# Normaliser and output gate in transposed squares of 32 by 32, and a written order for every engine and the transfer queue, in an mLSTM cell followed by a SwiGLU block

## Chip, cores and metric

One Trainium2 chip, one core. The time is device time in microseconds (us). The kernel before takes 761.7 us in the median of the four runs beside the changed kernel (760.92 to 761.99). Engines: PE is the matrix engine, DVE the vector engine, ACT the scalar engine, POOL is GpSimd, and SP is the engine whose queue issues nearly all transfers.

## The reference

An mLSTM cell (4 batches, 8 heads, 768 steps, head size 40), then a SwiGLU block on its 3072 tokens of 320 numbers. Weights arrive as float64 and are cut to float32 on the chip.

```python
# cell, per step t (m, f_stab, i_stab: running maximum and stabilised gates)
C = f_stab * C + i_stab * outer(vt, kt)
n = f_stab * n + i_stab * kt
y[:, :, t] = sigmoid(o_gate) * (C @ qt) / maximum(abs(n . qt), 1.0)
# block
g = x @ w_gate
out = (g * sigmoid(g) * (x @ w_val)) @ w_out        # 320 -> 1536 -> 320
```

## The kernel before

Time is cut in chunks of 128 steps: 24 units (batch and chunk) in 8 groups of three. For each unit, PE transposes k and q (`turn`) and multiplies them (`scores`). A weight matrix `w` is loaded (a running maximum, spread over all partitions), turned into decay weights (`weigh`), multiplied by the scores, and used in `attend`. Each attention also makes the new state C, which the next one needs; q is scaled by loaded factors e before it meets C. The normalised, gated result `x` is stored to memory and read back transposed as `xT`, the input of the block. A group's block has a hidden phase (12 steps, `gv_ps`, PE's largest work) and nine projection parts (`o_ps`), between which the next group's three `attend` stand. That stretch is the boundary. Weights are converted in 18 pieces during the start and group 0: 12 for the hidden products, 6 for `w_out`.

```python
tc_order = ctx.enter_context(tc.manual_schedule(engines={PE}))   # only PE's order is the program's
...
    def weigh(u):
        w = un["w"] = work.tile([128, H, L], F32, name="w_sb", bufs=2 * GC - 1)
        nc.sync.dma_start(out=w, in_=M_dram[b][c].unsqueeze(0).to_broadcast([128, H, L]))
        nc.vector.tensor_tensor(w, gb, w, op=ALU.subtract)
        nc.gpsimd.affine_select(w, w, ...)          # causal mask
        nc.scalar.activation(w, w, AF.Exp)
    ...
    def attend(u):
        ...                                         # products onto ys (PSUM), new state C
        for two in range(2):
            nc.vector.stream_shuffle(r[:, part], ys[two], mask=[ONE] * 32)   # denominator to 32 rows
            nc.vector.tensor_tensor(x[:, part], ys[two], un["o"][:, part], op=ALU.mult)
        nc.scalar.activation(r, r, AF.Abs)
        nc.vector.tensor_scalar(r, r, scalar1=1.0, scalar2=None, op0=ALU.max)
        nc.vector.reciprocal(r, r)                  # 128x512
        nc.vector.tensor_tensor(x, x, r, op=ALU.mult)
        ...                                         # four stores of x, two transposed reads into xT
    ...
        for u in after:                             # group after next: before the boundary, in program order
            weigh(u)
        follow = {-1: [(attend, nxt[0])], 1: [(attend, nxt[1])], 3: [(attend, nxt[2])]}
        for n in range(-1, 3 * GC):
            if n >= 0:
                project(g, *divmod(n, 3))
            for f, u in follow.get(n, ()):
                f(u)
```

## Time and profile before

| stretch, from the timeline of PE | us |
|---|---|
| start to the first hidden product of group 0 | 90.3 |
| the same of group 1 | 227.3 |
| periods of groups 1 to 5 | 80.2, 80.6, 79.6, 80.0, 76.5 |
| group 1's first hidden product to the end | 533.6 |

Read it as two parts: an uneven start up to 227 us and regular groups after it. The table of stretches shows both (per engine the busy us and the number of instructions, then granted clock, mean busy share of the 16 transfer engines, GB/s):

```profile
core 0: us, PE busy (x) PEld busy (x) DVE busy (x) ACT busy (x) POOL busy (x), PEclk, DMA share, GB/s
...
90.00:227.00 137.00, 96.13 (x512) 64.43 (x512) 104.67 (x135) 41.86 (x57) 39.29 (x29) 0.81 0.61 143
227.00:307.00 80.00, 74.64 (x512) 52.39 (x512) 41.54 (x70) 22.25 (x34) 9.47 (x10) 0.95 0.35 79
```

### The profile page before, as it was taken

To read this page: it belongs to the slowest core of one execution; us is meant where nothing else is said; L and a number is where in the kernel's file an instruction comes from. 1 tells how busy PE (TensorE), PEld (TensorE's weight loads), DVE (VectorE), ACT (ScalarE), POOL (GpSimd) and SP (SyncE) were. 2 spreads that over 40 slices of the span, in tenths; PEclk is the share of its full clock that TensorE was granted. 3 is DMA by queue.
4 is the path that set the end of the run, shared out by engine and by line. 5 is a ranking of instruction groups with operands and counts; after the bars stand their busy time and mean duration, and the time that the engine had idled before them with its cause. 6 is when DMAs were issued, how large, how long until landed. Compare 5 with 4: busy or idle time off the path is not lost.

```text
span 760.9 us, 10611 instructions
## 1 busy us (share of the span) xinstructions
PE 626.6 (82%) x4104; PEld 440.0 (58%) x4104; DVE 425.9 (56%) x659; ACT 193.0 (25%) x291; POOL 118.9 (16%) x129
## 2 busy tenths in 40 slices
PE   3244393668769998899969998999699999997998
PEld 3233362435547676566746666887476666675665
DVE  4689546999953476346814493449444844391330
ACT  2512131422333133211521243113321231110110
POOL 3252112533210111110100111101100101000000
PEclk9655596678889999899979998999899999998999
DMA  7775757655470046402640166007500220012000
GB/s 118 180 148 101 175 92 161 162 145 158 80 171 19 28 93 146 98 22 68 144 100 15 46 136 155 29 15 155 142 1 29 79 70 28 1 45 60 1 1 26
DMA packets 159954, 65.50 MB, mean 86 GB/s; under 512 B 106240, under 2 KB 152672, under 8 KB 159904
## 3 DMA queue, kind: packets, MB, share of 16 engines
q1 hardware_dynamic: 159904, 64.83, 36.8%
q8 instruction: 32, 0.52, 0.3%
q14 instruction: 18, 0.15, 0.1%
HBM read 56.75 MB, written 8.04 MB: 85 GB/s over the span
## 4 chain that ended last, share of the span: by engine, by line
PE 63%; DVE 11%; issue 11%; DMA 6%; POOL 3%; SPq 3%; ACT 2%; DVEq 0%; POOLq 0%; ACTq 0%
PE gv_ps L363 38%; PE o_ps L378 16%; PE yT L303 3%; DVE r_sb L339 3%; PE tp_kq L270 2%; PE sp L281 2%; DMA w_sb<-M_dram 2%; PE add L318 1%; DMA raw<-in_moe_w_val_dram 1%; DMA o<-in_o_gate_dram 1%; DMA xT<-x_dram 1%; DVE wo_sb L228 1%; DVE size L234 1%; POOL wgv_sb L235 1%; DVE wgv_sb L231 1%
## 5 line engine op out<-in xcount | busy, mean ns | idle before, releaser
L363 PE MATMUL gv_ps<-xT,wgv_sb 64*128 64x384 f32 x1920 | 359.3, 517 | 69.6 <-DVE sg L367 27.8
L363 PEld LDWEIGHTS gv_ps<-xT,wgv_sb 64*128 64x128 f32 x1920 | 229.0, 201 | 186.5 <-issue 53.1
L367 DVE TENSOR_TENSOR sg<-sg,gv_ps 128x384 f32<-128x384 f32 x96 | 53.1, 553 | 209.7 <-ACT sg L366 209.7
L378 PE MATMUL o_ps<-wo_sb,h_sb 128*128 128x320 f32 x576 | 167.3, 443 | 0.0
L378 PEld LDWEIGHTS o_ps<-wo_sb,h_sb 128*128 128x128 f32 x576 | 107.7, 193 | 42.5 <-issue 3.0
L366 ACT ACTIVATE sg<-gv_ps 128x384 f32<-128x384 f32 x96 | 47.1, 491 | 240.4 <-PE gv_ps L363 240.4
L339 DVE RECIPROCAL r_sb<-r_sb 128x512 f32<-128x512 f32 x24 | 80.3, 3344 | 0.6
L369 DVE TENSOR_TENSOR h_sb<-sg,gv_ps 128x384 f32<-128x384 f32 x96 | 53.1, 553 | 9.6 <-DVE sg L367 0.5
L257 DVE TENSOR_TENSOR w_sb<-g_T,w_sb 128x1024 f32<-128x1024 f32 x24 | 30.7, 1280 | 48.9 <-DMA w_sb<-M_dram 48.9
L291 POOL TENSOR_TENSOR qT<-qT,e_bc 128x512 f32<-128x512 f32 x20 | 27.4, 1372 | 176.8 <-PE sp L281 176.8
L258 POOL TENSOR_SCALAR_AFFINE_SELECT w_sb<-w_sb 128x1024 f32<-128x1024 f32 x24 | 28.4, 1184 | 156.1 <-DVE w_sb L257 133.8
L260 ACT ACTIVATE w_sb<-w_sb 128x1024 f32<-128x1024 f32 x24 | 25.4, 1057 | 107.5 <-POOL w_sb L258 107.4
L281 PE MATMUL sp<-qT,kT 64*128 64x128 f32 x384 | 33.5, 281 | 7.6 <-DVE w_sb L284 7.6
L281 PEld LDWEIGHTS sp<-qT,kT 64*128 64x128 f32 x384 | 32.6, 194 | 11.7 <-DVE w_sb L284 7.8
L303 PE MATMUL yT<-w_sb,v 128*64 128x128 f32 x384 | 30.0, 304 | 10.9 <-DVE w_sb L284 10.9
L284 DVE TENSOR_TENSOR w_sb<-sp,w_sb 128x512 f32<-128x512 f32 x48 | 31.0, 682 | 4.7 <-POOL v_w L263 4.7
L303 PEld LDWEIGHTS yT<-w_sb,v 128*64 128x64 f32 x384 | 23.2, 151 | 17.1 <-DVE w_sb L284 11.6
L318 PE MATMUL add<-v_w,k 128*64 128x48 f32 x320 | 20.5, 241 | 13.6 <-DVE x_sb L336 10.2
L133 DVE STREAM_TRANSPOSE oT<-o 128x512 f32<-128x512 f32 x24 | 26.4, 1114 | 8.9 <-ACT o L131 8.8
L337 ACT ACTIVATE r_sb<-r_sb 128x512 f32<-128x512 f32 x24 | 15.0, 627 | 55.3 <-DVE r_sb L335 55.3
L318 PEld LDWEIGHTS add<-v_w,k 128*64 128x64 f32 x320 | 19.6, 154 | 15.1 <-DVE x_sb L336 11.3
L235 POOL TENSOR_TENSOR wgv_sb<-wgv_sb,size 128x640 f32<-128x640 f32 x12 | 19.7, 1640 | 52.6 <-DVE size L234 51.8
(68 smaller groups left out, 422.2 us busy)
## 6 DMA issues: line engine op xcount, KB each, us to landing
w_sb<-M_dram SPq DMA_DIRECT2D x24, 512.0 KB
xT<-x_dram SPq DMA_DIRECT2D x48, 160.0 KB
e_bc<-e_dram SPq DMA_DIRECT2D x40, 128.0 KB
k<-in_k_dram SPq DMA_DIRECT2D x48, 80.0 KB
q<-in_q_dram SPq DMA_DIRECT2D x48, 80.0 KB
o<-in_o_gate_dram SPq DMA_DIRECT2D x48, 80.0 KB
raw<-in_moe_w_gate_dram SPq DMA_DIRECT2D x12, 320.0 KB
raw<-in_moe_w_val_dram SPq DMA_DIRECT2D x12, 320.0 KB
```

The source lines that it names most:

```text
L257: nc.vector.tensor_tensor(w, gb, w, op=ALU.subtract)
L258: nc.gpsimd.affine_select(w, w, compare_op=ALU.is_ge, fill=NEG, base=0, pattern=[[0, H], [1, L]], channel_multiplier=-1)
L281: nc.tensor.matmul(sps[two][:, j, :], lhsT=un["kT"][r, j, :], rhs=un["qT"][r, j, :], start=True, stop=True)
L284: nc.vector.tensor_tensor(w2, sps[two], w2, op=ALU.mult)
L303: nc.tensor.matmul(ys[two][col * HP:(col + 1) * HP, (h % PR) // 2, :], lhsT=lhsT, rhs=rhs, start=(two, col) in fresh, stop=last, skip_grou ...
L318: nc.tensor.matmul(add[two * DP:(two + 1) * DP, j], lhsT=un["k"][:, 2 * j + two, :], rhs=un["v_w"][:, h, :], start=(j == 0), stop=(j == PR ...
L339: nc.vector.reciprocal(r, r)
L363: nc.tensor.matmul(ps[i], lhsT=wgv_sb[r, kc, ts(m, 128)], rhs=xts[g][r, kc, :], start=(kc == 0), stop=(kc == NKC - 1))
L366: nc.scalar.activation(sg, ps[0], AF.Sigmoid)
L367: nc.vector.tensor_tensor(sg, sg, ps[0], op=ALU.mult)
L369: nc.vector.tensor_tensor(h, sg, ps[1], op=ALU.mult)
L378: nc.tensor.matmul(p, lhsT=hs[g, m][:, ts(i, 128)], rhs=wo_sb[:, m, :], start=(m == 0), stop=(m == NFC - 1))
```

## The change

The intent has two halves. First, the normaliser, now a step of its own called `finish`: the output is transposed in squares of 32 by 32, so that the denominator is one column of each square and its reciprocal is taken of 16 numbers per partition instead of 512; the output gate is applied in the same layout and needs no transpose of its own. Second, the order: before, a scheduler chose the order of DVE, ACT, POOL and SP; now the order of the program is the order of every engine, and the program is cut in small steps to say it. Output transfers move to ACT's queue, and weight pieces get three raw buffers instead of two.

```diff
-    tc_order = ctx.enter_context(tc.manual_schedule(engines={PE}))
+    ctx.enter_context(tc.manual_schedule(engines={PE, EN.DVE, EN.Activation, EN.Pool, EN.SP}))
...
+    def finish(u):
+        yb = work.tile([128, PR, NSQ, 32], F32, name="yb")
+        for two in range(2):
+            nc.vector.transpose(yb[:, two * PR // 2:(two + 1) * PR // 2], un["ys"][two]...)
+        nc.vector.scalar_tensor_tensor(den, in0=yb[:, :, :, ONE:], scalar=-1.0, in1=yb[:, :, :, ONE:],
+                                       op0=ALU.mult, op1=ALU.max)
+        nc.vector.tensor_scalar(den, den, scalar1=1.0, scalar2=None, op0=ALU.max)
+        nc.vector.reciprocal(den, den)
+        nc.vector.tensor_tensor(yb, yb, un["o"]..., op=ALU.mult)
+        nc.vector.tensor_tensor(yb, yb, den.to_broadcast([128, PR, NSQ, 32]), op=ALU.mult)
+        nc.vector.transpose(x.rearrange("p x (t four) -> p x four t", four=NSQ), yb)
+        ...                                         # stores of x, reads of xT, as before
...
+    load_v(first[2])
+    load_o(first[2])
+    for b in range(1, B):
+        spread(M_dram, M_sb, b)                     # maxima and e factors of batches 1 to 3 to memory
+        spread(e_dram, e_sb, b)
+    gates_scope.close()
+    conv = conv_scope.enter_context(tc.tile_pool(name="conv", bufs=2))   # takes the gates' memory
...
+        for n, u in enumerate(nxt):
+            follow[2 * n - 1] = [(attend, u), (finish, u)]
+        for n, u in enumerate(after):
+            follow.setdefault(2 * n - (n < 2), []).append((load_w, u))
+            follow.setdefault(2 * n, []).append((weigh, u))
+            follow.setdefault(n + 4, []).append((turn, u))
+            follow.setdefault(n + 5, []).append((weigh_exp, u))
+        for n in range(-1, 3 * GC):
             if n >= 0:
+                need(NFC + 2 * (n + 1))             # w_out pieces, two ahead of their projection part
                 project(g, *divmod(n, 3))
```

## The prediction

> **What bounds the kernel now.** I read the busy shares and slices first. They say the matrix engine (PE) works 82% of the span, but not evenly.
>
> ```profile
> PE 626.6 (82%) x4104; PEld 440.0 (58%) x4104; DVE 425.9 (56%) x659; ACT 193.0 (25%) x291; POOL 118.9 (16%) x129
> ...
> PE   3244393668769998899969998999699999997998
> DVE  4689546999953476346814493449444844391330
> PEclk9655596678889999899979998999899999998999
> ```
>
> There are two regimes. In the first 12 slices (up to 227 us) PE is a third to three quarters busy at a low clock and DVE is full from 120 to 220 us; afterwards PE is nearly full with a dip about every 80 us. The chain of waits dates this: the first `gv_ps` of the eight groups starts at 90.3, then 227.3, 307.5, 388.1, 467.7, 547.7, 624.2 and 696.1. So the first part takes 227.3 us, and the periods are 80.2, 80.6, 79.6, 80.0, 76.5, 71.9 and a last group of 64.8.
>
> Next the groups that the change touches, with mean ns after the busy time:
>
> ```profile
> L339 DVE RECIPROCAL r_sb<-r_sb 128x512 f32<-128x512 f32 x24 | 80.3, 3344 | 0.6
> L133 DVE STREAM_TRANSPOSE oT<-o 128x512 f32<-128x512 f32 x24 | 26.4, 1114 | 8.9 <-ACT o L131 8.8
> L337 ACT ACTIVATE r_sb<-r_sb 128x512 f32<-128x512 f32 x24 | 15.0, 627 | 55.3 <-DVE r_sb L335 55.3
> L335 DVE STREAM_SHUFFLE r_sb<-yT 128x256 f32<-128x256 f32 x48 | 21.1, 443 | 0.0
> L336 DVE TENSOR_TENSOR x_sb<-yT,oT 128x256 f32<-128x256 f32 x48 | 17.8, 398 | 0.0
> L340 DVE TENSOR_TENSOR x_sb<-x_sb,r_sb 128x512 f32<-128x512 f32 x24 | 17.6, 733 | 0.3
> ```
>
> Last, a dip: the SP queue and DVE where group 1 ends, then PE, from the timeline (start, duration).
>
> ```profile
> 301.28 0.58 SPq L255 DMA_DIRECT2D w_sb<-M_dram  x1
> 302.02 1.25 SPq L352 DMA_DIRECT2D xT<-x_dram  x2
> ...
> 306.70 1.23 DVE L257 TENSOR_TENSOR w_sb<-g_T,w_sb 128x1024 f32<-128x1024 f32 x1 [9.06 <-DMA w_sb<-M_dram]
> ...
> 307.49 2.92 PE L363 MATMUL gv_ps<-xT,wgv_sb 64*128 64x384 f32 x7 [3.95 <-DMA o<-in_o_gate_dram]
> ```
>
> A `w_sb` transfer is usable 5.4 us after its issue begins, `xT` 5.5. PE waits there for `xT`, the input of the next group. The named releaser, an o gate, is a transfer counted on the same wait; `xT` is what is read.
>
> Write T for the end of the first attention (`attend`) of the next group on PE, just after the last `gv_ps`. Here T = 272.7, so T to the next group is 34.8 us. The others, read the same way, are 33.8, about 33.5, 33.1 and 30.6. With no wait it would be 27: nine projection parts of 2.2, two attentions of 2.3, three turns of 0.87 to 0.9.
>
> **What the Trainium skill says.** "TensorE: Matmul & The Clock Gate", Part 1, says an idle window drops PE to half clock and that about 3.4 us of work lifts it. The windows of this trace agree: granted clock 0.50 from 308 to 311 after that dip, 1.00 from 314. I charge 2.3 us per dip. The same page, section "Architectural detail", says DVE and ScalarE are strict first in, first out; no case here contradicts it, and everything below rests on it. "DMA: Bandwidth & Descriptors", "Anatomy of one DMA", puts the fixed part near 2 us, mostly the receipt of the last write; its fit is for another issuing path. The trace's least loaded `xT` (issued 693.09, matmul at 696.08) takes 2.95. "VectorE: DVE Perf Modes", "First, the fixed hardware budget", says the reciprocal is an iterative divide with a repeat count of 8; the trace has 3344 ns against 733 for a multiply of that size.
>
> **The change part by part.**
>
> Normaliser. Old DVE work per unit: 2 x 0.443 + 2 x 0.398 + 0.447 (the maximum) + 3.344 + 0.733 + 1.114 = 7.3 us, plus ScalarE's 0.63 between. New: two transposes of 128x256, estimated at half of 1.11 plus a start, 1.2; three operations on 16 elements, 0.2 each by the 0.15 us copies of 4 or 5 elements plus a wait, 0.6; two 128x512 multiplies 0.73 each; one transpose 1.11; small waits. Sum 4.4. That is 2.9 us less DVE work per unit, 70 us over 24 units. Most lies beside PE; on the path it is 24 shorter tails of about 2.4 us, if nothing comes between.
>
> Weights. The same five DVE operations for each of 18 pieces (about 4.7 us a piece before). The first now writes a contiguous tile, so it and the mask should cost 0.49 rather than 0.81, as the `wo_sb` pieces did: 0.5 us less a piece. Three raw buffers replace two. Five pieces move behind the first hidden phase.
>
> Start. I walk the written order with the durations above. DVE reaches the first piece near 17 us, the weights of attention near 27 (behind piece 1), the first finish near 42 to 46. Then a new wait: the e factors of unit 2 are issued after unit 0's x stores and xT reads (1.6 + 1.4 landing + 1.3), so they land near 55. GpSimd does that unit's qT ahead of unit 1's `kept`, and DVE stands at C until 57. Rest: 1.8 + 4.4 + 1 + 2.6 + 4.4, then 6 to `xT`. First hidden near 78 instead of 90.
>
> Group 0. DVE per step: gating 1.15, piece about 4, weighing and scoring 0.65; 5.8 us or slightly less. Transfers: a raw piece 2.8 (640 KB near 230 GB/s, seen from 30 to 35 us) plus a third of k, q, v, o and e, 2.4, so 5.2. Both are near full, so I take 6.5 with misses: T near 160 instead of 186. The boundary carries five pieces and gets longer: 48 instead of 41. Second hidden phase near 208 instead of 227: a gain of 19.
>
> Boundaries 1 to 5, the decisive part. The listed order on DVE is finish 0, weigh 0, C 1, finish 1, weigh 1, (C 2), finish 2. On the transfer queue it is x 0, xT 0, w 0, x 1, xT 1, w 1, x 2, xT 2, w 2. So weigh 0 needs a transfer that cannot be issued until finish 0 has been stored and landed, and finish 1 stands behind weigh 0. From x done to w landed: four stores 1.55, landing 1.4 (as from 683.11 to 684.52), two xT issues 1.27, w 4.4 (85.06 to 89.43; 5.4 at worst): 8.7. On GpSimd `kept` 1 stands behind the mask of w 0. The chain from T:
>
> finish 0 4.5 + 8.7 + weigh 1.2 + mask 1.1 + kept 0.6 + C 0.5 + finish 1 4.5 + 8.7 + weigh 1.2 + finish 2 4.5 + store, land and load 5.9 = 41.4; where a C 2 exists another 2.2, so 43.6 on three of the five.
>
> Sum over five: 214 against 166 before, plus 48. PE's second attention waits too (C 1 at 16.7 against 11.4), inside this chain. Up to 1 us more each: the last copy of z stands on ScalarE behind exp of w 2, and the second hidden product waits for its bank: plus 3. The boundary from 6 to 7 has no weighing: its stall of 4 us and the half clock after it vanish, minus 6.
>
> Output transfers on ScalarE's queue. They free SP from waits for z (87 us in the queue's waits, mostly idle time). On the path they help only at the boundary from 6 to 7, counted above.
>
> Sum: 761.6 - 19 + 48 + 3 - 6 = 787. Several latencies above are from crowded moments. Taking w at 4.0 and a finish at 4.2 removes 0.8 + 0.9 from each of five boundaries, 8 us. I put the prediction between: 782.
>
> **Rivals.**
>
> First: the written order removes the dips, the author's intent. For it: x is ready 2.4 us sooner, outputs no longer stand before `xT`, and the weights of attention are spread. Then each period falls from 80 towards 71 and the time to about 690. Against: weighing w 0 cannot precede the landing of w 0, and the listed queue has it behind xT 0.
>
> Second: the start decides. DVE is full there, so 0.5 us on 18 pieces, 2.9 on 6 units and a third buffer could put the second hidden phase at 190, a gain of 37; with quick transfers at the boundaries (37.5 each, plus 22) the time is near 740. For it: DVE idled 10.7 us for a raw piece near 110 to 120 us while transfers for later groups went first. Against: the start's own waits for e and for xT.
>
> Third: transfers of group 0 become the bound. The order there is strict, three raw pieces deep, and a waiting one stops all behind it. Then T of group 0 is near 180, nothing is gained there, and the time is near 805.
>
> **Range and chances.** The boundary estimate is off by perhaps 12 us in all, group 0 by 15, both ways: 782, with 754 to 810 eight times in ten. Faster by over 2% (below 746) needs rival one or two: 0.12. Within 2%: 0.31. Slower by over 2% (above 777): 0.57.
>
> **What would show it.** Reciprocal groups of 128x16 near 0.2 us and DVE busy time near 345 us show the normaliser right. First hidden near 78 and second near 208 show the start right. At each of the next five boundaries DVE should stand before the weighing (`w_sb<-g_T,w_sb`) twice, some 8 to 9 us each, released by `w_sb<-M_dram`, with T to the next `gv_ps` at 41 to 44; periods near 88. The boundary from 6 to 7 should show no stall. The prediction is wrong if `w_sb` is issued or lands before the finish ahead of it is done, if DVE passes the weighing without waiting, or if group 0 gains over 35 us.

## More of the kernel before

In group 0 DVE works 104.7 of 137 us; in a later group it works half of the time. There PE waits mainly at the boundary, and DVE's waits for `w` (us in total, times, longest) are already there:

```profile
DVE w_sb L257 <- DMA w_sb<-M_dram: 48.9, 8, 9.1
```

## The result, and the profile after

The changed kernel takes 829.32 us in the median of four runs (827.25 to 832.84), against 761.7. The ratio is 1.0894, with a 95% interval of 1.0851 to 1.0937: slower. (A ratio here is the mean time of one kernel's fast runs over that of the other's in the same rounds, so not quite the quotient of the two medians.)

The page after, its busy line and slices:

```profile
PE 630.8 (76%) x4104; PEld 421.2 (51%) x4104; DVE 341.7 (41%) x614; ACT 161.7 (20%) x255; POOL 110.4 (13%) x128
...
PE   4033277671499978899769976997879976999998
...
DVE  4075247876524343243324522433324332444230
```

DVE lost 84 us of work and PE stands idle more: four of the first five digits are 3 or less, and the later dips take more of the span. The normaliser did what it should (busy us, mean ns of one, then the idle time before it):

```profile
L400 DVE STREAM_TRANSPOSE x_sb<-yb 128x512 f32<-128x512 f32 x24 | 26.3, 1094 | 0.8
L390 DVE STREAM_TRANSPOSE yb<-yT 128x256 f32<-128x256 f32 x48 | 18.9, 429 | 6.2 <-PE yT L357 6.2
...
L396 DVE RECIPROCAL den<-den 128x16 f32<-128x16 f32 x24 | 6.1, 253 | 0.8
```

The reciprocal went from 3344 to 253 ns, and a whole finish takes 4.0 us in the stretch below (291.39 to 295.37). So where did the time go? By stages:

| | before | predicted | after |
|---|---|---|---|
| first hidden product, group 0 | 90.3 | 78 | 104.2 |
| from it to T (end of the next group's first attention) | 95.9 | 82 | 79.0 |
| T to the first hidden product, group 1 | 41.1 | 48 | 64.1 |
| first hidden product, group 1 | 227.3 | 208 | 247.3 |
| from it to the end of the span | 533.6 | 579 | 578.2 |

Of the 64.6 us between the two profiled spans (760.9 and 825.5), 44.6 come after group 1's first hidden product and 20.0 before it.

**A later boundary.** This is group 1 to group 2, from the timeline: the queue, then DVE, then PE (start, duration, what; in brackets the idle time before and what ended it).

```profile
295.40 2.48 SPq L408 DMA_DIRECT2D x_dram<-x_sb  x4
299.27 1.27 SPq L412 DMA_DIRECT2D xT<-x_dram  x2
300.59 0.60 SPq L294 DMA_DIRECT2D w_sb<-M_dram  x1
```
```profile
294.27 1.10 DVE L400 STREAM_TRANSPOSE x_sb<-yb 128x512 f32<-128x512 f32 x1
304.71 1.22 DVE L309 TENSOR_TENSOR w_sb<-g_T,w_sb 128x1024 f32<-128x1024 f32 x1 [9.34 <-DMA w_sb<-M_dram]
307.61 0.36 DVE L377 TENSOR_TENSOR C<-add,kept 128x192 f32<-128x192 f32 x1 [1.67 <-POOL kept L376]
...
320.89 1.23 DVE L309 TENSOR_TENSOR w_sb<-g_T,w_sb 128x1024 f32<-128x1024 f32 x1 [8.85 <-DMA w_sb<-M_dram]
```
```profile
308.32 1.38 PE L357 MATMUL yT<-qT,C 64*64 64x128 f32 x16 [5.62 <-DVE C L380]
...
334.03 6.16 PE L423 MATMUL gv_ps<-xT,wgv_sb 64*128 64x384 f32 x16 [7.13 <-DMA xT<-x_dram]
```

The first finish ends at 295.4. Its stores and the reads of `xT` go out, and only then, at 300.59, the load of `w`. DVE stands 9.34 us before `weigh`. Behind `weigh` on DVE stands C of the second attention, so PE's third attention, which needs it, waits 5.62 us (308.32). The second finish comes only after that C, and behind it the same happens again (8.85 us). PE starts the next group 7.13 us after it has run out of work.

**The start.** DVE's first weight piece, and the end of the queue's first round of loads:

```profile
38.27 0.30 SPq L248 DMA_DIRECT2D M_dram<-M_sb  x1
38.61 0.30 SPq L248 DMA_DIRECT2D e_dram<-e_sb  x1
```
```profile
15.36 0.24 DVE L281 COPY dec<-dec_ps 128x80 f32<-128x80 f32 x1 [4.79 <-PE dec_ps L279]
40.64 0.49 DVE L169 TENSOR_SCALAR top<-raw 128x640 uint32<-128x640 uint32 x1 [25.04 <-DMA e_dram<-e_sb]
```

DVE is idle from 15.6 to 40.6 us. The piece's data have nothing to do with `e_dram`; its output tile does. The pool `conv` was opened in the memory of the gates' pool, and the tile seems to lie where `e_sb` or its neighbours lay (no view shows the addresses). So it may be written only when the transfers that read the gates are done, and those for batches 1 to 3 stand last in the queue, behind all loads of v, o and raw weights.

The waits of the start and of the first boundary:

```profile
PE tp_kq L326 <- DMA k<-in_k_dram: 20.2, 3, 17.6
```
```profile
PE o_ps L438 <- POOL wo_sb L185: 29.7, 5, 9.1
```

The first is one wait of 17.6 us for the second group's k, ahead of the first hidden product in PE's order; the second are PE's waits for converted pieces of `w_out` while group 0 is projected.

### The profile page after: what moved, and what is told of

It is laid out like the page before. It is cut to its first block, busy times and chain, and to the rows that moved or that the text cites. A ratio compares the mean times of both kernels' runs of the same rounds, so it can differ in the third digit from the quotient of the medians.

```text
span 825.5 us, 10494 instructions
## 1 busy us (share of the span) xinstructions
PE 630.8 (76%) x4104; PEld 421.2 (51%) x4104; DVE 341.7 (41%) x614; ACT 161.7 (20%) x255; POOL 110.4 (13%) x128
## 4 chain that ended last, share of the span: by engine, by line
issue 36%; PE 36%; DVE 9%; DMA 8%; POOL 7%; SPq 2%; ACT 1%; POOLq 0%; DVEq 0%
PE gv_ps L423 25%; PE o_ps L438 7%; DMA w_sb<-M_dram 2%; POOL w_sb L310 2%; PE sp L336 2%; DMA x_dram<-x_sb 2%; DMA e_bc<-e_dram 2%; DVE x_sb L400 1%; POOL qT L345 1%; SPq L408 1%; POOL wgv_sb L185 1%; DMA xT<-x_dram 1%; SPq L412 1%; DVE top L171 1%; DVE size L183 1%
## 5 line engine op out<-in xcount | busy, mean ns | idle before, releaser
L423 PE MATMUL gv_ps<-xT,wgv_sb 64*128 64x384 f32 x1920 | 353.8, 513 | 59.8 <-DMA xT<-x_dram 35.7
L423 PEld LDWEIGHTS gv_ps<-xT,wgv_sb 64*128 64x128 f32 x1920 | 208.5, 200 | 190.7 <-issue 37.4
L438 PE MATMUL o_ps<-wo_sb,h_sb 128*128 128x320 f32 x576 | 172.4, 452 | 29.7 <-POOL wo_sb L185 29.7
L438 PEld LDWEIGHTS o_ps<-wo_sb,h_sb 128*128 128x128 f32 x576 | 109.7, 197 | 78.3 <-POOL wo_sb L185 33.2
L309 DVE TENSOR_TENSOR w_sb<-g_T,w_sb 128x1024 f32<-128x1024 f32 x24 | 31.0, 1297 | 156.1 <-DMA w_sb<-M_dram 156.1
L357 PE MATMUL yT<-qT,C 64*64 64x128 f32 x320 | 18.2, 338 | 39.8 <-DVE C L380 36.0
L357 PE MATMUL yT<-w_sb,v 128*64 128x128 f32 x384 | 37.9, 326 | 0.0
L357 PEld LDWEIGHTS yT<-qT,C 64*64 64x64 f32 x320 | 12.3, 164 | 49.4 <-POOL kept L376 38.8
L442 ACT COPY z_sb<-o_ps 128x320 f32<-128x320 f32 x24 | 10.1, 421 | 126.0 <-PE o_ps L438 126.0
L328 ACT COPY kT<-tp_kq 128x512 f32<-128x512 f32 x24 | 13.8, 575 | 98.6 <-PE tp_kq L326 98.6
L326 PE MATMUL tp_kq<-ident,k 128*128 128x128 f32 x96 | 16.9, 305 | 20.6 <-DMA k<-in_k_dram 20.2
L357 PEld LDWEIGHTS yT<-w_sb,v 128*64 128x64 f32 x384 | 31.1, 166 | 1.0 <-issue 1.0
```

The source lines that it names most:

```text
L357: nc.tensor.matmul(ys[two][col * HP:(col + 1) * HP, (h % PR) // 2, :], lhsT=lhsT, rhs=rhs, start=(two, col) in fresh, stop=last, skip_grou ...
L423: nc.tensor.matmul(ps[i], lhsT=wgv_sb[r, kc, ts(m, 128)], rhs=xts[g][r, kc, :], start=(kc == 0), stop=(kc == NKC - 1))
L438: nc.tensor.matmul(p, lhsT=hs[g, m][:, ts(i, 128)], rhs=wo_sb[:, m, :], start=(m == 0), stop=(m == NFC - 1))
```

## The experiments

Each run is timed in three rounds against the kernel before. All gave correct results. "First" and "second" are the starts of the first hidden product of groups 0 and 1 in the profiled run; "gap" is from the end of a group's last hidden product to the next group's first (2.3 us longer than from T at the first boundary). Some of the expectations below say T where they mean this gap.

| run | median us | ratio to before | first | second | gap 0 to 1 | periods 1 to 5 |
|---|---|---|---|---|---|---|
| before | 761.7 | 1 | 90.3 | 227.3 | 43.4 | 76.5 to 80.6 |
| changed | 829.3 | 1.0894 | 104.2 | 247.3 | 66.4 | 86.7 to 90.2 |
| e1_spread | 817.4 | 1.0742 | 91.4 | 235.9 | 67.5 | 88.0 to 91.5 |
| e2_kq | 826.2 | 1.0855 | 97.1 | 244.5 | 66.9 | 86.5 to 90.4 |
| e3_w | 730.6 | 0.9587 | 106.1 | 247.0 | 66.8 | 70.5 to 70.7 |
| e6_eager | 833.1 | 1.0940 | 104.5 | 252.7 | 65.1 | 88.2 to 90.9 |
| e8_three | 715.5 | 0.9375 | 85.2 | 231.7 | 67.0 | 70.5 to 70.7 |
| e9_conv | 703.7 | 0.9232 | 85.0 | 218.7 | 54.0 | 70.5 to 71.1 |
| e10_more | 699.7 | 0.9173 | 91.3 | 215.6 | 54.6 | 70.5 to 70.7 |
| e12_turn_first | 701.1 | 0.9200 | 83.7 | 218.0 | 54.5 | 70.5 to 70.9 |
| e14_weigh | 754.1 | 0.9907 | 105.3 | 248.9 | 66.8 | 72.0 to 78.3 |
| e5_norm_in_before | 740.3 | 0.9716 | 89.7 | 209.6 | 30.9 | 79.4 to 80.6 |
| e11_sp_free | 710.2 | 0.9318 | 86.7 | 230.7 | 63.7 | 70.5 to 70.7 |
| e4_pe_only | 710.0 | 0.9317 | 76.2 | 191.0 | 41.7 | 76.2 to 78.7 |
| e15_pe_dve | 722.3 | 0.9496 | 84.7 | 233.5 | 63.6 | 70.5 to 72.9 |
| e16_dve_free | 707.4 | 0.9293 | 83.1 | 209.1 | 46.3 | 70.7 to 76.0 |
| e17_switch | 679.5 | 0.8935 | 78.1 | 195.1 | 38.8 | 70.5 to 70.7 |

Theory at the outset: the normaliser gains, the written order loses, at three places in the start and at every boundary by the load of `w`. The main rival was that other waits stand right behind these, so that removing one gives little.

### The load of w (e3_w)

```diff
-            follow.setdefault(2 * n - (n < 2), []).append((load_w, u))
+            if n < 2:
+                more.setdefault(10, []).append((load_w, u))               # hidden phase
+            else:
+                follow.setdefault(-1, []).insert(0, (load_w, u))          # ahead of the first finish
```

> Theory (at each boundary the load of w stands in the transfer queue behind the stores of x, these wait for the finish, and weigh on the in-order DVE waits for the load, so that the next finish waits for weigh): with w of two units loaded in the hidden phase and the third ahead of the first finish's stores, the DVE waits for w of some 8 to 11 us each (156 us in 18 waits) fall to under 20 us, the periods of groups 1 to 5 fall from 88 to 90 us to 71 to 76, and the time falls by 65 to 90 us, to 740 to 765. The start does not move (first hidden chunk 104 us). Rival (other waits at the boundary take their place: finish, transposed store and load of x, eviction of scores): periods stay over 82 us and the time falls by less than 35 us.

Measured: 730.57 us, ratio 0.9587 (0.9559 to 0.9614), 99 us less than the changed kernel, and the start unmoved. It beats the expected range: no wait for `w` is left on DVE in the whole trace. The same place of the same boundary now (start, duration; no bracket means no wait):

```profile
293.68 1.11 DVE L400 STREAM_TRANSPOSE x_sb<-yb 128x512 f32<-128x512 f32 x1
294.64 1.21 DVE L309 TENSOR_TENSOR w_sb<-g_T,w_sb 128x1024 f32<-128x1024 f32 x1
297.52 0.36 DVE L377 TENSOR_TENSOR C<-add,kept 128x192 f32<-128x192 f32 x1 [1.67 <-POOL kept L376]
```

`weigh` follows the finish at once, C comes 3.8 us after the finish's last step starts instead of 13.3, and from T to the next hidden product it is 26.5 or 27.2 us, which the prediction had named as the time without a wait (27). The rival falls. The gain is not waiting alone: from group 1's first hidden product (cut at 247 us) to the end, PE was busy 510.4 of 578 us at a mean granted clock of 0.93 in the changed kernel, and 479.4 of 482 us at 1.00 here. So of the 96 us, 65 are waits and 31 are the same products taking less time.

### Which order makes the loss, the queue's or DVE's (e14_weigh)

```diff
-            follow.setdefault(2 * n, []).append((weigh, u))
+            follow.setdefault(2 * n + 2, []).append((weigh, u))
```

> The changed kernel with the loads of w left where they are, behind the stores of x, and only the DVE step that reads w moved: one finish later. Theory (the loss is made by two orders together, the queue's and DVE's: DVE stands at weigh for w, and the next finish stands behind weigh): the same gain as with the loads moved, periods of groups 1 to 5 of 71 to 76 us and 735 to 755 us. Rival (it is the late landing of w itself, or the load on the transfer queue, that holds the boundary): periods stay over 82 us, over 790 us.

Measured: 754.05 us (750.85 to 761.24), ratio 0.9907 (0.9851 to 0.9964). The loads stay behind the stores of `x`, and moving one DVE step gives back 75 of the 99 us. So the larger part is made by the two orders together: late `w` alone would not have stopped the finishes. The time lies at the upper end of its expected range, and the periods (up to 78.3) pass theirs. What is left shows behind the boundary. The third `weigh` still waits (7.26 us at 398.4), its exponential follows on ACT, and behind that in ACT's order stands the last copy of z, whose bank the second hidden product needs:

```profile
400.89 1.06 ACT L316 ACTIVATE w_sb<-w_sb 128x1024 f32<-128x1024 f32 x1 [6.54 <-POOL w_sb L310]
401.85 0.41 ACT L442 COPY z_sb<-o_ps 128x320 f32<-128x320 f32 x1
```
```profile
402.31 4.86 PE L423 MATMUL gv_ps<-xT,wgv_sb 64*128 64x384 f32 x17 [2.37 <-ACT z_sb L442]
```

PE waits so 12.0 us in six times, 0.5 to 3.0 us each. After this one the granted clock is near 0.5 for some 3.5 us, as the table of stretches shows:

```profile
402.30:404.00 1.70, 1.69 (x6) 1.01 (x8) 0.00 (x0) 1.27 (x1) 0.57 (x1) 0.57 0.81 212
404.00:406.00 2.00, 2.00 (x8) 1.03 (x6) 1.11 (x2) 0.50 (x2) 0.00 (x0) 0.51 0.23 46
406.00:408.00 2.00, 2.00 (x23) 1.56 (x21) 0.55 (x1) 1.09 (x2) 0.00 (x0) 1.00 0.48 115
```

The same follows three others of the six waits (1.77, 2.70 and 3.01 us; half clock for 3.4, 6.8 and 6.8 us), but not the two shortest (0.47 and 1.71 us). An estimate from these: 12.0 us of waits, and half of the 19.1 us that PE worked at a clock of 0.50, 9.6 us, make 22 of the 28 us by which groups 1 to 6 of this profiled run (the slowest of its four) are longer than those of e3_w.

### The three places in the start

**Reused memory (e1_spread).** The six spreads go right behind those of batch 0.

```diff
     spread(e_dram, e_sb, 0)
+    for b in range(1, B):
+        spread(M_dram, M_sb, b)
+        spread(e_dram, e_sb, b)
     load_v(first[0])
```

> Theory (the start waits on reused memory): the first weight piece writes into memory that the gates held, and so waits for the spreads of batches 1 to 3, which stand last in the start's queue and end at 40.6 us. With these six spreads issued right behind the first batch's, before the loads of v and o, the first piece's DVE step starts near 20 to 27 us instead of 40.64, and the first hidden chunk near 86 to 92 us instead of 104.2; the time falls by 12 to 18 us (ratio to before about 1.07). Rival (the loads of v and o or raw weights end the start anyway): the first hidden chunk moves by less than 4 us. Rival (a later wait takes it over before the second group): the first hidden chunk comes earlier, but the second group's (247.3 us in the changed kernel) moves by less than half of that.

Measured: 817.4 us, 11.9 less, ratio 1.0742 (1.0711 to 1.0772). The first hidden product is 12.8 us earlier, group 1's 11.4. DVE's wait for the reused memory fell from 25.0 to 6.1 us, and its first piece starts at 22.45 us. Theory held; the time gain lies just under the expected 12 to 18 us. That the wait came from the old contents' transfers is thereby shown: only their place in the queue was changed.

**The second group's k and q (e2_kq).** Their loads go ahead of the first stores of `x`.

```diff
     attend(first[0])
+    for r in range(GC, NRK):
+        pads(r)
+    for u in second:
+        load_kq(u)
     scores(first[2])
```

> Theory (the queue's order delays the turns that stand before the first hidden chunk on PE): the second group's k and q loads are issued behind the last stores of x of group 0, and PE waits 17.6 us for them. Issued ahead of these stores, that wait goes and the first hidden chunk starts 6 to 9 us earlier, near 96 us instead of 104.2; the time falls by 6 to 9 us. Rival (the stores of x and the transposed loads are moved back by as much as the loads that now stand ahead of them): the first hidden chunk moves by less than 3 us.

Measured: 826.22 us, ratio 1.0855 (1.0811 to 1.0900), so no difference in time that is resolved from the changed kernel. The wait did go: first hidden product 97.1, 7.1 us earlier, and what it waits for is now `xT` (12.64 us, with the turns done at 84.5). But group 1's came only 2.8 us earlier: the next stretch, which runs at the pace of converted pieces, took back the rest (why it did was not tested). The chunk was predicted right and the time wrong.

**The raw loads of w_out (e6_eager).** Each raw load is issued with the step that frees its buffer.

```diff
             made[0] += f is piece_b
+        while todo and todo[0][0] is piece_load:
+            f, i = todo.pop(0)
+            f(i)
```

> Theory (the raw loads of the last three weight pieces stand behind group 1's first x, xT and w): loads that follow a piece are issued at once with it rather than at the next call, so they reach the queue before the stores of x where the buffers allow it; PE's waits for the last pieces of w_out (29.7 us) fall by 6 us or more, and the first boundary (64.1 us from T of group 0 to the second group's first hidden chunk) by 6 to 10 us; the time falls by as much. Rival (the raw buffers, three of them, decide when the loads can go, not the place of the call): less than 3 us.

Measured: 833.07 us (ratio 1.0940), no gain. My theory of the first boundary fell: PE's waits for `w_out` were 29.1 us instead of 29.7. The timeline shows why. The last two pieces' conversions stand on DVE behind the second finish, which stands behind the second attention on PE, which stands behind products that wait for earlier pieces. The transfer was not what ended the wait.

**The three moves together (e8_three),** e1, e2 and e3:

> The three moves that gained alone, together: the spreads early, k and q of the second group early, and w of the group after next before the stores of x. Theory (they are waits at different places and add up): first hidden chunk near 84 us (104.2 - 12.8 - 7.1), the second group's near 234 to 238 (the stretch between is not touched by these moves, and took back part of either gain alone), then periods of 70.6 us as with the w move alone: 711 to 722 us. Rival (they are the same wait seen twice): first hidden chunk over 89 us, or no earlier second group than 240; 724 us or more.

Measured: 715.46 us, ratio 0.9375. First 85.2, second 231.7 (a little before the expected 234 to 238), periods 70.5 to 70.7: they add up.

**The order of conversions (e9_conv),** on top of these, the last pieces ahead of the second finish:

```diff
-                need(NFC + 2 * (n + 1))
+                need(NP)                           # all 18 pieces at n = 0
```

> As the three moves together, and the last weight pieces converted ahead of the second group's second finish instead of behind it. Theory (in the first boundary the last two pieces stand on DVE and GpSimd behind that finish, which waits for an attention that stands on PE behind the products that wait for the earlier pieces, so that PE's waits for w_out, 29.7 us, come from the order and not from the transfers: issuing the raw loads earlier had no effect): T of group 0 to the second group's first hidden chunk falls from 67 us to 50 to 57, and the time by 10 to 16 us against the three moves. Rival (raw loads or the conversion's own work of 3.5 us a piece on DVE set it): under 4 us.

Measured: 703.65 us, ratio 0.9232. The gap went from 67.0 to 54.0 and the time down by 11.8 us. In the window of this boundary (160 to 235 us), first e8_three, then e9_conv:

```profile
PE o_ps L438 <- POOL wo_sb L185: 28.8, 6, 9.4
```
```profile
PE o_ps L438 <- POOL wo_sb L185: 19.4, 5, 8.5
```

So the in-order chain of DVE and PE was the cause of most of it, and 19.4 us of waits for conversions stay.

**More conversions in DVE's idle time (e10_more, e12_turn_first).** Five steps right behind group 0's last finish (`fill(5)`), and the same behind the second group's turns.

> As the run before, and up to five more conversion steps on DVE right behind the last finish of group 0, where DVE has nothing to do until the first hidden chunk. Theory (group 0's hidden phase, 75 us against 41.6 of the later groups, is held by conversions one piece ahead of PE; what is converted ahead shortens it): the hidden phase of group 0 falls by 5 to 12 us and the first hidden chunk stays within 2 us; the time falls by 4 to 12 us. Rival (the transfers of that stretch, whose 16 engines are 79% busy, hold it): less than 3 us.

> As the run with five more conversion steps, but these behind the second group's turns, so that ScalarE's squares do not stand ahead of the copies that free the banks of the turns (PE waited 18.7 us for these copies, and the first hidden chunk moved from 85.0 to 91.3). Theory: the first hidden chunk goes back to 84 to 87 us, and the time falls by 3 to 6 us, to 693 to 697. Rival (the conversions end no earlier, and PE waits for the pieces in the hidden phase instead): within 2 us.

Measured: 699.68 us (696.4 to 701.36) and 701.12 us (699.8 to 702.59). For e10_more group 0's hidden phase (first product to the last one's end) fell from 79.7 to 69.7 us, but the first hidden product moved from 85.0 to 91.3, because PE's turns waited 18.7 us for copies that stood on ACT behind the new conversions. Moving the steps cured that (83.7) and gained nothing: the rival of e12_turn_first holds, the pieces come no earlier and PE waits for them later. Both gains over e9_conv are small or unresolved.

### The halves of the change apart

**The normaliser alone, in the kernel before (e5_norm_in_before).** `finish` as above, the gate without its transpose, four gate buffers; the order stays as it was.

> The kernel before with the new normaliser and gate alone, and its own order otherwise. Theory: DVE's busy time falls by some 70 us (24 units by about 3), and as DVE was only 55% busy but stood in the boundary's chain with its finish of 7.3 us a unit, the time falls by 3 to 9 us a boundary in six boundaries at most, by 5 to 20 us in all. Rival (the boundary is bound by the second attention and the transfers of x whatever the finish takes): within 4 us. If it were the normaliser that makes the change slower: above 770 us.

Measured: 740.32 us, ratio 0.9716 (0.9692 to 0.9739): 22 us faster, just over the expected range. DVE's busy time fell from 425.9 to 357.6 us. The gain lies in the start (second 17.7 us earlier) and in the last two groups (7 us); the periods of groups 1 to 5 did not move. There the gap fell to 29.0 us while the hidden phase grew to some 50: what is gained at the boundary comes back as PE waiting for DVE's gating step (54.2 us in 11 waits). So the rival of no gain holds for the regular groups, the theory for the start.

**The order left to the scheduler, in the changed kernel (e4_pe_only, e11_sp_free).** One line each: the set of engines with a written order is PE alone, or all but SP.

```diff
-    ctx.enter_context(tc.manual_schedule(engines={PE, EN.DVE, EN.Activation, EN.Pool, EN.SP}))
+    ctx.enter_context(tc.manual_schedule(engines={PE}))                                        # e4
+    ctx.enter_context(tc.manual_schedule(engines={PE, EN.DVE, EN.Activation, EN.Pool}))        # e11
```

> The changed kernel with PE's order written as before the change and every other engine and the queue left to the scheduler: the new normaliser with an order of the old kind. Theory (the normaliser gains some 22 us, as it did alone in the kernel before, and the written orders of the others lose 89): 725 to 765 us. Rival (the program's other moves, such as piecewise gates, lose by themselves): over 790 us.

> The changed kernel with the order of the transfer queue left to the scheduler and those of the four engines written. The build shows that the scheduler issues the loads of w in the hidden phases, ahead of the stores of x, for most units. Theory: periods of groups 1 to 5 fall to 71 to 78 us as with the three loads moved by hand, and the time to 720 to 765 us. Rival (the written orders of the engines alone lose, whatever the queue does): over 790 us.

Measured: 709.99 us (ratio 0.9317) and 710.22 us (0.9318), both better than expected. Without the written orders the changed kernel is 6.8% faster than the kernel before; with them it is 8.9% slower. The 30 us between e5_norm_in_before (740.3) and e4_pe_only (710.0) belong to the rest of the change: the smaller steps and their places in the program, the third raw buffer, the output transfers on ACT's queue. No run takes these apart. Freeing the transfer queue alone is enough for even periods of 70.6, because the scheduler issues most loads of `w` before the stores of `x`. But its start stays slow (230.7), while e4_pe_only has the best start (191.0) and periods of 76 to 79.

**Which engine's order holds the start (e15_pe_dve, e16_dve_free).** Written: PE and DVE; or PE, ACT and POOL.

> The changed kernel with PE's and DVE's order written, ScalarE, GpSimd and the queue left to the scheduler. Theory (DVE's order holds the start: it is the engine whose pieces, finishes and weighing interleave): the second group's first hidden chunk comes at 222 to 235 us, as with only the queue free (230.7). Rival (ScalarE's and GpSimd's orders hold it): at 191 to 205 us.

> The changed kernel with PE's, ScalarE's and GpSimd's order written, DVE and the queue left to the scheduler. Theory (DVE's order holds the start): the second group's first hidden chunk at 191 to 205 us. Rival (ScalarE's and GpSimd's orders hold it): at 220 to 235 us.

Measured: group 1's first hidden product at 233.5 and 209.1. With e11_sp_free and e4_pe_only this is a table of two by two, the queue free in all four:

| | ACT and POOL written | ACT and POOL free |
|---|---|---|
| DVE written | 230.7 | 233.5 |
| DVE free | 209.1 | 191.0 |

With DVE's order written, freeing the others gains nothing. With DVE free it gains 18 us more. DVE's order is what holds the start first; e16_dve_free came later than its theory said, because ACT's and POOL's orders hold it next. DVE's busy us in the first 40 us show the difference: the changed kernel, e15_pe_dve, e16_dve_free, e4_pe_only (the columns are those of the table of stretches):

```profile
0.00:40.00 40.00, 8.32 (x64) 6.28 (x64) 9.49 (x24) 5.41 (x8) 2.98 (x21) 0.78 0.88 164
```
```profile
0.00:40.00 40.00, 11.70 (x64) 8.99 (x64) 10.36 (x26) 9.97 (x14) 5.24 (x31) 1.00 0.91 171
```
```profile
0.00:40.00 40.00, 11.69 (x64) 8.99 (x64) 14.59 (x33) 6.10 (x10) 5.15 (x22) 1.00 0.95 169
```
```profile
0.00:40.00 40.00, 20.61 (x160) 16.70 (x160) 24.35 (x54) 12.06 (x15) 13.81 (x39) 0.94 0.91 164
```

The third figure after the first comma is DVE's: 9.5, 10.4, 14.6 and 24.4 us. The wait for reused memory is 25.0, 22.1 and 15.7 us in the first three and 0.4 in e4_pe_only.

**Each order where it is better (e17_switch).** Only PE written through the start and group 0, everything written from group 1 on, with the loads of `w`, the spreads, the k and q loads and the conversions as in e9_conv.

```diff
+    order = ExitStack()
+    order.enter_context(tc.manual_schedule(engines={PE}))
...
             conv_scope.close()
             raw_scope.close()
+            order.close()
+            ctx.enter_context(tc.manual_schedule(engines={PE, EN.DVE, EN.Activation, EN.Pool, EN.SP}))
```

> The scheduler for all engines but PE in the start and group 0, the written order with the loads of w moved from group 1 on. Theory (the written order loses in the start, where work is uneven, and wins in the even groups once the w loads stand right): second group's first hidden chunk at 185 to 200 us, then periods of 70.6 us: 668 to 685 us, under every run so far (best 699.7). Rival (the switch from one order to the other costs a wait or leaves buffers late): over 695 us.

Measured: 679.47 us (679.21 to 681.06), ratio 0.8935 (0.8899 to 0.8970), the fastest of all, with the second at 195.1 and periods of 70.5 to 70.7. Its page, and its stretch from group 1 on:

```profile
PE   4423478955999999999999999999999999999998
```
```profile
195.00:677.00 482.00, 479.48 (x3361) 317.52 (x3360) 204.56 (x393) 105.71 (x180) 51.24 (x54) 1.00 0.31 74
```

PE is busy 479.5 of 482 us at full clock. There the orders have nothing left to give.

## Why the prediction was wrong, point by point

The direction was right and the size was not: 782 told, 829.3 measured, outside the range of 754 to 810. The step that failed is the start, "Second hidden phase near 208 instead of 227: a gain of 19". It came at 247.3, a loss of 20. Of the 39 us of this error, 26 lie before the first hidden product of group 0 and 16 in the boundary from group 0 to 1; 3 were gained between.

- **Normaliser: right.** A finish of 4.4 was told, 4.0 measured; DVE busy near 345 told, 341.7 measured. Alone it gains 22 us (e5_norm_in_before), which the prediction never put together as a figure of its own.
- **Boundaries 1 to 5: right.** T to the next hidden product was told as 41.4 or 43.6, 214 in all, and measured as 42.7, 40.5, 42.6, 41.6 and 41.4, 209 in all. DVE waits twice or more per boundary for `w`, up to 10.7 us (18 waits, 156.1 us). e3_w and e14_weigh show the chain. What waits on PE is the third attention of the group (the second after T). From group 1's first hidden product to the end, 579 was told (787 less 208) and 578.2 measured. That this agrees to 1 us is in part luck: against the kernel before, boundaries 1 to 5 cost 44 us where 48 were told, the hidden phases of groups 1 to 6 cost 8 where 3 were told, and the stall and slow clock from 6 to 7 gave 7 back where 6 were told. The 5 us that I then took off for quicker transfers were not there. Two readings of the trace before are slightly off, with no weight in the sum: the third boundary is 32.7, not about 33.5, and the least loaded `xT` took 2.99, not 2.95.
- **Boundary 6 to 7: right,** no stall.
- **First hidden product near 78: wrong by 26.** "DVE reaches the first piece near 17 us" was the error. It reached the piece and stood until 40.6, because the tile's memory was still being read by transfers at the queue's end. e1_spread is worth 12.8 us there. The walk also missed that the second group's k and q stand behind the last stores (e2_kq, 7.1 us). With both, 85.2; there DVE still waits 6.9 us for the reused memory and 5.4 us for a raw piece ahead of its second. The e factors that I did name as a wait were one (12.3 us on POOL), but DVE stood at C until 74.7 us, not 57.
- **Group 0's hidden phase: right to 3 us,** 82 told and 79.0 measured.
- **Boundary 0 to 1: 48 told, 64.1 measured.** I had charged five pieces of work, and not that conversion, finish, attention and projection form one chain through in-order engines. e9_conv takes 13.0 of the 16 us away; my first explanation, the queue, fell with e6_eager.
- **Rivals.** The first (the order removes the dips, periods near 71, time near 690) is what the written order gives once `w` is loaded in time: e8_three and e9_conv lie at 715 and 704, above it, with periods of 70.5 to 71.1. My argument against it was right for the order as written. The second did not occur. The third came closest in number (T near 180, 805 us; T was 183.2), but not for its cause: from 104 us to T the transfer engines were 71% busy, and no conversion on DVE waited for a raw piece. T is late since everything began late, not since group 0 ran longer.

Open: the last 7 us before the first hidden product (85.2 against 78), of which the two waits just named are candidates; the last 3 of the 16 us at the first boundary, and what in DVE's free order, beyond the missing wait for reused memory, brings group 1's first hidden product to 191.0 us (e4_pe_only) where the best order by hand has 215.6 (e10_more).

## What to carry to other kernels

A load that a strictly ordered engine will wait for must be issued before anything in the queue that waits for that same engine. Otherwise queue and engine take turns (here 18 waits on DVE, 156.1 us). When an order is written by hand, walk it per engine and per queue together, and look for tiles whose memory a closed pool left behind: here their first writer waited for the last transfer that read the old contents (25.0 us). Where work is uneven (a start), a scheduler's order may be better than a written one (group 1 began at 195.1 us in e17_switch, and at 215.6 in the best start written by hand); where it is regular, a written order can keep the bound engine full (479.5 of 482 us).

## What the Trainium skill lacked or had wrong

- "TensorE: Matmul & The Clock Gate", Part 1, gives one idle window of about 3.4 us as what drops the clock. In e14_weigh a gap of 2.37 us was enough: the clock granted was 1.00 up to its end, 0.57 and 0.51 in the next 3.7 us, then 1.00. A gap of 1.77 us was enough once too, and one of 1.71 us was not.
- No page that I read says that memory reused from a closed pool makes its first writer wait for transfers that still read it. Here that was a wait of 25.0 us on DVE, named by the profile with the old tile's transfer.
- None warns of a transfer queue and an in-order engine that wait for each other in turn. Here it was 156.1 us of DVE's waits in 18 times, and moving three loads per group took 99 us off the time.
- None gives the time of a DVE reciprocal by size. Here it is 253 ns for 128x16 and 3344 ns for 128x512.
